# Sparse attention and a softplus feed-forward layer on one core: the second batch's attention in one TensorE visit a head pair, its masks on VectorE, and a new order of the first 140 microseconds

## The chip, the cores and the metric

The kernel runs on 1 core of one Trainium2 chip. The metric is device time in microseconds; the kernel before takes 890.61 us (median of 3 runs, 890.55 to 891.92). In the profile PE is TensorE, DVE VectorE, ACT ScalarE, POOL GpSimd and SP SyncE, which issues nearly all DMAs.

## The reference

Eight batches of eight heads, 576 tokens, head dimension 64. Heads 0 to 3 attend to the last 32 keys, heads 4 to 7 to earlier keys of the same class modulo 32. The attention output, 4608 tokens of 512 features, goes through a feed-forward layer with softplus:

```python
scores = scale * np.matmul(q, k.transpose(0, 1, 3, 2))
mask_local = (rel >= 0) & (rel < stride)
mask_strided = (rel >= 0) & (pos[None, :] % stride == pos[:, None] % stride)
scores = np.where(masks[None, :, :, :], scores, -1000000000.0)
attn = np.exp(scores - np.max(scores, axis=-1, keepdims=True))
attn = attn / (np.sum(attn, axis=-1, keepdims=True) + 1e-09)
x = attn @ v                      # to 4608 x 512
h = x @ w_in                      # 512 x 2048
g = np.maximum(h, 0.0) + np.log1p(np.exp(-np.abs(h)))
out = g @ w_out                   # 2048 x 512
```

All of it is float32; q and k are drawn so large that the softmax is sharp.

## The kernel before

**Pairs.** Two heads share the 128 partitions, so a batch is four pairs. Pair n is numbered through: 0 to 3 are the first batch, 4 to 7 the second, 8 and up the rest. For a pair: load q and k (`q`, `k`), lay q out in blocks with zeros between the two heads (`D`, a copy of half the partitions each), scores by matmuls of 64 columns (`S`, parts 0 and 1, six and three chunks of 64 keys), maxima (`X`), exponentials (`E`), sums, guard and reciprocals (`r`, `R`), normalisation (`M`), transposes of the probabilities, product with v (`V`, two halves), and the result split into a high and a low part (`H` on ScalarE, `L` on VectorE) that are stored as the columns of x.

**The exponentials** come in two forms. A narrow part takes one ScalarE instruction for each 64-wide chunk, with the maximum as bias (`x` prepares it) and the sum as a by-product. A wide part (named in `WIDE`, line 74) subtracts the maxima on VectorE (`Y`), takes one ScalarE instruction (`E`) and sums on VectorE (`Z`).

**Masks.** In batches 0 and 1 TensorE adds the masks: four matmuls of the identity with a mask tile a pair (line 340). From batch 2 on VectorE adds the mask while it moves the scores out of PSUM (`add_mask`, line 416).

**Transposes** of the first batch go over TensorE (`T`, three a pair) and are copied out of PSUM (`C`); all later ones are 16 VectorE stream transposes a pair (`P`, line 457).

**Feed-forward.** Tokens go in 9 chunks of 512. For chunk c and each of 16 blocks f of 128 hidden features: `F`, 12 matmuls of 512 columns (`hidden`, line 629: four column groups of x times high and low parts), three ScalarE passes (`A`, `Ae`, `Al`), softplus on VectorE (`u`), a high and a low part of the result (`Gh`, `Gl`), and `O`, 12 matmuls that add to four PSUM banks `py` (`output`, line 669). Each 128x512 block of weights arrives as 64-bit numbers (`wi`, `wo`) and is prepared once: `a` on ScalarE, `B` and `d` on VectorE, high part `h`, low part `l`.

**PSUM.** `ps_h` has two buffers, used by `F` (held until `u`), by `T` and by half of a joint product; `ps_o` and `ps_s` have one each.

**Order.** Up to the middle of the second chunk the order is written out by hand as the list `FIRST` (line 35): every engine gets its instructions, and SyncE its DMAs, in the order of the list; `ON_POOL`, `ON_VECTOR` and `ON_SCALAR` (lines 62 to 72) give the engine of the tasks that may go to several. `Fa` is the part of a hidden block that needs only the first three pairs, `F` then the rest. `Q`, `QA` and so on are the first two hidden blocks of chunk 1 (`Q` 0 and 1). Behind the list everything is ordered by the class `Plan`, from costs and due times: there one visit a pair (`S`) on TensorE does the scores of pair n, part 0 in `ps_s` and part 1 in `ps_o`, and the products of pair n-1 (`sums_of`).

In the second batch the four score parts and product halves of a pair are separate tasks of the list: TensorE goes there for S40, S41, S50, S51 with V40, V41 with S60, V50 with S61, V51 with S70, S71 with V60, V61, V70 and V71.

Of the kernel before, what the change touches and what calls it, by code (L numbers as in the profile page):

```python
# [18 lines left out]
P = 128  # L19
# [18 lines left out]
X20 T01 C01 Bo0 D30 v0 R1 do0 V00 H00 T02 C02 L00 Y20 M1 k3 S31 X31 E21 E20 Z20 V01 li0 wi1  # L38
S30 H01 L01 ai1 Bi1 r2 di1 x31 R2 M2 wi3 ai3 T10 C10 T11 C11 v1 T12 ho0 lo0 Bi3 V10 T21 X30 Y30
di3 C12 H10 L10 V11 E30 T20 E31 Z30 C21 H11 v2 L11 r3 R3 M3 C20 T22 wi2 ai2 Bi2 V20 C22  # L40
H20 L20 di2 hi3 li3 T32 k4 wo1 C32 wi9 T31 ao1 T30 C31 v3 C30 hi1 li1 V21 H21 wo2 ao2 L21 V31 wi4
V30 Bo1 Bo2 ai9 H31 L31 Fa0 q4 H30 L30 F0 wi10 do1 Bi9 di9 wo3 Fa1 hi2 li2 D4 S40 A0
Ae0 Al0 ho1 lo1 ao3 F1 u0 Gh0 X40 x40 F2 Bo3 Gl0 ai4 Bi4 hi9 li9 di4 do2 ho2 v4 A1 E40 S41
X41 x41 wi5 ai5 q5 Bi5 Ae1 Al1 u1 wo15 D5 lo2 O0 wi6 hi4 di5 li4 F3 Gh1 Gl1 O1 A2 Ae2 wi8 ai8
do3 ai10 k5 E41 S50 r4 hi5 wo12 Bi8 li5 Al2 A3 di8 u2 R4 Ae3 M4 Al3 wi7 ai7 wi12 hi8 X50
x50 F4 u3 Gh3 Bi10 di10 F5 Gh2 Gl2 wo5 wo4 ho3 lo3 E50 P4 O2 A4 Gl3 q6 hi10 ao5 Bo5 Ae4 Al4
u4 wi11 S51 A5 Ae5 li8 X51 li10 ai6 Al5 Bi7 di7 V40 H40 x51 Gh4 Gl4 E51 r5 F8 hi7 do5 u5 ao4
# [71 lines left out]
def attention_softplus_ffn(  # L119
# [201 lines left out]

    def scores(n, part):

        b = order[n][0]
        masked = b < 2
        if b == 0:
            ps = py[2 * (n % 2) + part]
        elif b == 1 or part == 0:
            taken.append(n)
            ps = ps_s.tile([P, 512], F32, tag="ps", name=f"ps_{n}_{part}")  # L330
        else:
            shared[n] = ps_o.tile([P, 512], F32, tag="po", name=f"po_{n}")
            ps = shared[n][:, S // 2 :]
        pss[n, part] = ps
        lo, hi = SPLIT[part]
        rows = [slice(64 * place, 64 * place + 64) for place in range(2)]

        def add(first):
            for place in range(2):
                nc.tensor.matmul(  # L340
                    ps[rows[place], : 64 * (hi - lo)],
                    lhsT=ident_b[:, rows[place]],
                    rhs=mask_of(n, part),
                    start=first,
                    stop=not first,
                )


        if masked and n > 0:
            add(True)  # L350
        for x in range(lo, hi):
            for place in range(2):
                a, i = block_at(x, place)
                c = TILE * a + 32 * i
                nc.tensor.matmul(  # L355
                    ps[rows[place], 64 * (x - lo) : 64 * (x - lo) + 64],
                    lhsT=blocks_of(n)[:, c // 32].rearrange("p h l -> p (h l)"),
                    rhs=k_of(n)[:, c : c + 64],
                    start=not masked or n == 0 and x == lo,
                    stop=not masked or n > 0 and x == hi - 1,  # L360
                )
        if masked and n == 0:
            add(False)
# [144 lines left out]
    def weighted(n, half, joint=False):  # L508


        if joint:
            if half == 0:
                po = shared[n + 1]
            else:
                po = ps_h.tile([P, 512], F32, tag="ph", name=f"pv_{n}")
        elif half == 1 and (n == NPAIR - 1 or n >= 2 * NPAIR):
            taken.append(n)
            po = ps_s.tile([P, 512], F32, tag="ps", name=f"pv_{n}_{half}")
        else:
            po = ps_o.tile([P, 512], F32, tag="po", name=f"pv_{n}_{half}")  # L520
        pos[n, half] = po
        for x in range(NTILE // 2):
            a = NTILE // 2 * half + x
            for h in range(2):
                nc.tensor.matmul(  # L525
                    po[64 * h : 64 * h + 64, TILE * x : TILE * x + TILE],
                    lhsT=vs[n][:, a, h, :],
                    rhs=pt_of(n, a)[:, h, a % 2],
                    start=True,
                    stop=True,  # L530
                )
# [170 lines left out]
    def of(name, usual):  # L702
# [7 lines left out]
    first["W"] = lambda: dummies(10)  # L710
    for n in range(2 * NPAIR + 2):
# [288 lines left out]
```

## Time and profile before

| what | value |
|---|---|
| time, median of 3 runs | 890.61 us (890.55 to 891.92) |
| span of the profiled execution, first to last instruction | 890.1 us |
| busy: TensorE | 879.0 us, 99% |
| busy: VectorE | 576.6 us, 65% |
| busy: ScalarE | 445.8 us, 50% |
| busy: GpSimd | 64.0 us, 7% |
| granted TensorE clock | 1.0 |
| DMA | 58.27 MB, mean 65 GB/s |

The page gives the profiled execution's own time as its span and no other. Busy shares are means over stages of different kinds: in the first tenth of the span ScalarE is at 9 tenths and the DMA engines above 5, in the last tenth both are at 3 or less. The views that are used are the windows (busy time of each engine in a stretch of time), the chain of waits (the work that ended last, followed back), the timelines of single engines, and the groups of instructions by line.

### The profile page before, as it was taken

The numbers are of one execution on the slowest core, as the hardware profiler recorded it, in microseconds if no ns is written. First come the engines' busy times: TensorE is split into PE (matmuls) and PEld (weight loads), VectorE is DVE, ScalarE is ACT, GpSimd is POOL, SyncE is SP. The second block draws the span as 40 slices with busy tenths as digits, with TensorE's granted clock in tenths as the row PEclk, the third lists the DMA queues.
The fourth block names the chain that finished last, engine by engine and source line by source line (L and its number), as shares of the span: only waits on it lengthen the run. The fifth ranks groups of instructions, "written<-read, shape, count | busy, mean of one in ns | idle before, by whom it ended". The sixth has DMA issues, their size and how long they took to land.

```text
span 890.1 us, 14332 instructions
## 1 busy us (share of the span) xinstructions
PE 879.0 (99%) x5634; PEld 723.6 (81%) x5634; DVE 576.6 (65%) x1268; ACT 445.8 (50%) x796; POOL 64.0 (7%) x93
## 2 busy tenths in 40 slices
PE   7999999999999999999999999999999999999998
PEld 5778888888888888888888888888888888888886
DVE  7878877788766777776766676677777333333332
ACT  7999665554544445445445454445543333333332
POOL 7254350000000000000000000000000000000000
PEclk9999999999999999999999999999999999999999
DMA  9856202121211122111211121111200010001001
GB/s 337 314 205 209 93 18 76 56 75 45 91 37 30 36 74 62 44 45 32 92 44 45 44 92 30 30 43 54 81 18 18 1 48 1 0 1 48 1 1 48
DMA packets 50083, 58.27 MB, mean 65 GB/s; under 512 B 3168, under 2 KB 35296, under 8 KB 50016
## 3 DMA queue, kind: packets, MB, share of 16 engines
q1 hardware_dynamic: 49728, 57.03, 19.5%
q8 instruction: 44, 0.72, 0.3%
q10 hardware_dynamic: 288, 0.33, 0.1%
q14 instruction: 23, 0.19, 0.1%
HBM read 47.91 MB, written 9.44 MB: 64 GB/s over the span
## 4 chain that ended last, share of the span: by engine, by line
PE 96%; ACT 2%; DMA 1%; DVE 1%; issue 0%; ACTq 0%
PE py L669 44%; PE ph L629 44%; PE ps L355 3%; PE pv L525 2%; PE po L525 1%; PE po L355 1%; DMA kT<-in_qk_dram 1%; PE idle L692 0%; ACT early_l L399 0%; ACT early_h L264 0%; ACT a_i L589 0%; ACT x_h L563 0%; ACT early_l L264 0%; PE py L355 0%; PE ps L340 0%
## 5 line engine op out<-in xcount | busy, mean ns | idle before, releaser
L669 PE MATMUL py<-w_o,gh 128*128 128x512 f32 x1152 | 358.4, 392 | 0.0
L629 PE MATMUL ph<-x_h,w_i 128*128 128x512 f32 x1152 | 355.5, 390 | 0.0
L641 ACT ACTIVATE u<-ph 128x512 f32<-128x512 f32 x144 | 86.3, 599 | 399.0 <-PE ph L629 398.6
L629 PEld LDWEIGHTS ph<-x_h,w_i 128*128 128x128 f32 x1152 | 215.7, 188 | 45.2
L669 PEld LDWEIGHTS py<-w_o,gh 128*128 128x128 f32 x1152 | 213.9, 188 | 46.4
L669 PE MATMUL py<-w_o,gl 128*128 128x512 f32 x576 | 224.1, 389 | 0.0
L629 PE MATMUL ph<-x_l,w_i 128*128 128x512 f32 x576 | 224.1, 389 | 0.0
L650 DVE SCALAR_TENSOR_TENSOR u<-ph,u 128x512 f32<-128x512 f32 x144 | 99.3, 690 | 178.3 <-ACT u L646 176.3
L457 DVE STREAM_TRANSPOSE pt<-prob 32x192 f32<-32x192 f32 x448 | 137.1, 314 | 6.4
L669 PEld LDWEIGHTS py<-w_o,gl 128*128 128x128 f32 x576 | 108.1, 188 | 22.8
L629 PEld LDWEIGHTS ph<-x_l,w_i 128*128 128x128 f32 x576 | 108.2, 188 | 22.6
L662 DVE TENSOR_TENSOR gl<-u,gh 128x512 fp32r<-128x512 f32 x136 | 94.3, 694 | 12.8 <-ACT gh L264 2.2
L644 ACT ACTIVATE u<-u 128x512 f32<-128x512 f32 x144 | 91.3, 634 | 4.3
L646 ACT ACTIVATE u<-u 128x512 f32<-128x512 f32 x144 | 91.1, 633 | 4.4
L264 ACT COPY qT<-prob 64x576 f32<-64x576 f32 x56 | 70.6, 1261 | 0.3
L264 DVE CAST gh<-u 128x512 fp32r<-128x512 f32 x128 | 54.5, 426 | 10.9 <-DVE u L650 0.5
L416 DVE TENSOR_TENSOR prob<-ps,mask_b 128x384 f32<-128x384 f32 x24 | 13.4, 558 | 50.0 <-PE ps L355 50.0
L355 PEld LDWEIGHTS ps<-kT,qT 128*64 128x64 f32 x720 | 24.0, 137 | 9.0 <-issue 8.5
L355 PE MATMUL ps<-kT,qT 128*64 128x64 f32 x720 | 27.6, 225 | 0.3 <-DMA kT<-in_qk_dram 0.3
L561 DVE TENSOR_TENSOR x_l<-pv,x_h 128x288 fp32r<-128x288 f32 (+2 forms) x47 | 18.8, 412 | 9.0 <-ACT x_h L563 8.9
L447 DVE TENSOR_TENSOR prob<-prob,st 128x576 f32<-128x576 f32 x27 | 21.9, 811 | 0.9
L525 PE MATMUL pv<-pt,v_in 128*64 128x96 f32 x396 | 22.1, 248 | 0.0
(100 smaller groups left out, 481.7 us busy)
## 6 DMA issues: line engine op xcount, KB each, us to landing
v_in<-in_v_dram SPq DMA_DIRECT2D x28, 320.0 KB, 3.5
out_dram<-o SPq DMA_DIRECT2D x35, 256.0 KB, 2.2
ri<-in_moe_w_in_dram SPq DMA_DIRECT2D x16, 512.0 KB, 7.3
ro<-in_moe_w_out_dram SPq DMA_DIRECT2D x16, 512.0 KB, 7.7
kT<-in_qk_dram SPq DMA_DIRECT2D x28, 288.0 KB, 2.9
prob<-in_qk_dram SPq DMA_DIRECT2D x28, 288.0 KB, 2.7
v_in<-in_v_dram SPq DMA_DIRECT2D x28, 48.0 KB, 2.7
room<-in_v_dram SPq DMA_DIRECT2D x4, 320.0 KB, 6.6
```

The source lines that it names most:

```text
L264: (engine.copy if engine is nc.scalar else engine.tensor_copy)(dst, src)
L355: nc.tensor.matmul(ps[rows[place], 64 * (x - lo) : 64 * (x - lo) + 64], lhsT=blocks_of(n)[:, c // 32].rearrange("p h l -> p (h l)"), rhs=k ...
L447: engine.tensor_tensor(pv, pv, rc.unsqueeze(2).broadcast_to(pv.shape), op=ALU.mult)
L457: nc.vector.transpose(pt[32 * (i + c) : 32 * (i + c) + 32, h, a : a + hi - lo, 32 * i : 32 * i + 32,], src[:, lo:hi, 32 * c : 32 * c + 32],)
L525: nc.tensor.matmul(po[64 * h : 64 * h + 64, TILE * x : TILE * x + TILE], lhsT=vs[n][:, a, h, :], rhs=pt_of(n, a)[:, h, a % 2], start=True, ...
L629: nc.tensor.matmul(ph, lhsT=w32["i", f][:, half, cc * P : (cc + 1) * P], rhs=x_of(x, cc)[:, t0 : t0 + n], start=(i == 0), stop=(i == 3 * N ...
L641: nc.scalar.activation(us[c, f], phs[c, f], AF.Abs)
L644: nc.scalar.activation(u, u, AF.Exp, scale=-1.0)
L646: nc.scalar.activation(u, u, AF.Ln, bias=1.0)
L650: nc.vector.scalar_tensor_tensor(u, in0=phs.pop((c, f)), scalar=0.0, in1=u, op0=ALU.max, op1=ALU.add)
L662: engine.tensor_tensor(g, us.pop((c, f)), ghs[c, f].bitcast(F32), op=ALU.subtract)
L669: nc.tensor.matmul(py[t], lhsT=g[:, sl], rhs=w32["o", f][:, half], start=(f == 0 and n == 0), stop=(f == NFC - 1 and n == 2),)
```

## The change

The list `FIRST` and the lists of engines are replaced; nothing in `Plan` changes. In words:

- Second batch: the masks are added by VectorE (`Y`, `add_mask`), not by TensorE; one maximum over all nine chunks (`X4` for pair 4), one preparation of the bias (`s4`), nine narrow exponentials from SBUF. One task `J` does both score parts of a pair and the products of the pair before it; pair 7's products stay `V70` and `V71`.
- First batch: wide parts are 00, 10, 20, 30, 01 and 21 in place of 00, 11, 20 and 30.
- Hidden blocks 0 to 3 are cut into `Fa` and `F`, before only 0 and 1.
- The second half of the products of pairs 0 to 3 and 7 goes to `ps_s`, before of pair 3 and of those from 8 on.
- The zeros for the layout of pair 4's q are a task (`z4`) and no longer part of the setup; the layouts of pairs 4 to 8 are two tasks each, so that the halves can go to different engines.
- Engines: 35 tasks on GpSimd (33 before), 42 on VectorE (29 before); the order of all tasks is new.

```diff
-W mask q0 D00 k0 D01 S00 X00 Y00 q1 D11 S01 X01 E00 x01 Z00 k1 D10 S11 X11 q2 D20 Y11 E01 r0 wi0
-S10 X10 D21 x10 k2 S21 ai0 wo0 q3 D31 S20 R0 M0 E10 Bi0 di0 X21 hi0 E11 T00 x21 C00 ao0 Z11 r1
...
+q0 k0 mask D00 W q1 q2 k1 D01 k2 D11 S00 D21 S01 D10 X00 X01 D20 q3 Y00 E00 Y01 S10 z4 E01 X10 Z00
+Z01 D30 k3 S11 X11 D31 r0 S21 Y10 S20 wi0 x11 R0 M0 S30 T00 X21 E10 X20 wi2 ai0 T01 E11 v0 Z10 Y20
+r1 Y21 X30 E20 v2 C00 C01 R1 Z20 M1 E21 ai2 Y30 Z21 S31 T02 V00 C02 X31 E30 H00 r2 v1 Bi0 wi1 T11
+T10 C11 Bi2 C10 R2 x31 Z30 V01 L00 T12 E31 di0 V10 H01 ai1 C12 L01 M2 T20 T21 r3 v3 R3 C20 H10 M3
+hi0 V11 Bi1 wi3 T22 C21 T31 wi4 H11 C22 L10 L11 di1 C31 wo2 hi1 V20 V21 k4 wi5 T30 wo0 T32 di2 ai3
+H20 H21 L20 C30 L21 C32 li1 q4 ao2 li0 V30 V31 H31 hi2 wi15 ai4 Bi3 di3 Fa0 wo1 Bi4 wi8 li2 hi3 L31
+H30 ai5 q5 L30 F0 di4 hi4 Bi5 Fa1 A0 Ae0 Bo2 wi6 D40 li3 Al0 ao0 wo5 F1 u0 li4 di5 D41 A1 do2 Ae1
+Bo0 wi11 Fa2 Al1 do0 Gh0 J4 ho2 hi5 ho0 wo4 u1 F2 Y41 lo2 li5 lo0 Gl0 ao1 D50 Y40 A2 ai6 Bo1 Fa3 k6
+Gh1 Ae2 wi9 Al2 ai8 X4 do1 wo8 Gl1 O0 u2 ao5 Bo5 F3 s4 wo9 Bi8 k5 E4 wo3 v4 wi7 ho1 Bi6 A3 Gh2 lo1
+do5 Ae3 F4 Al3 D51 Gl2 di6 di8 ho5 wo7 r4 hi6 O1 R4 hi8 u3 F5 li8 ao4 M4 Gh3 P4 A4 Gl3 wi10 Ae4 Al4
+u4 Bo4 wi13 A5 O2 do4 Ae5 Al5 li6 ai7 Bi7 J5 ao3 Bo3 q6 u5 v5 wo14 lo5 ho4 di7 F8 H41 do3 Gh5 Y50
+Y51 Gh4 wi14 hi7 ao8 wi12 Gl5 li7 X5 O5 L41 ho3 H40 ao7 lo4 A8 ai11 lo3 Bo8 F6 Ae8 s5 Bo7 do8 Gl4
+Al8 Bi11 ai9 D60 wo10 di11 E5 wo6 u8 hi11 A6 r5 Ae6 do7 Gh8 Bi9 ho8 Al6 F7 L40 R5 M5 Gl8 di9 lo8 O4
+wo11 u6 ai10 li11 ho7 A7 D61 Ae7 O3 P5 hi9 ai12 Al7 lo7 ao6 J6 Bi12 Bo6 di12 H51 li9 u7 do6 H50 Y61
...
 WIDE = """
-00 11 20 30
+00 10 20 30 01 21
 """.split()
...
-    for n in range(NPAIR + 1):
-        zeros(n)
+    for n in range(NPAIR):
+        zeros(n, nc.vector if n < 2 else nc.gpsimd)
...
-        b = order[n][0]
-        masked = b < 2
-        if b == 0:
+        masked = n < NPAIR
+        if masked:
             ps = py[2 * (n % 2) + part]
-        elif b == 1 or part == 0:
+        elif part == 0:
...
+    def row_exponentials(n):
+
+        pv, _, (mx, sm, _, _) = parts(n)
+        for a in range(NCHK):
+            nc.scalar.activation(
+                pv[:, a],
+                pv[:, a],
+                AF.Exp,
+                bias=mx[:, a : a + 1],
+                scale=SCALE,
+                accum_out=sm[:, a : a + 1],
+            )
...
-        elif half == 1 and (n == NPAIR - 1 or n >= 2 * NPAIR):
+        elif half == 1 and (n < NPAIR or n >= 2 * NPAIR - 1):
...
+    def joint_scores(n):
+
+        scores(n, 0)
+        scores(n, 1)
+        if n > NPAIR:
+            for half in range(2):
+                weighted(n - 1, half, True)
...
+            task(f"J{n}", joint_scores, n)
+            for j in range(2):
+                task(f"Y{n}{j}", add_mask, n, j)
+            task(f"X{n}", row_maxima, n)
+            task(f"s{n}", bias_of, n, None, of(f"s{n}", nc.vector))
+            task(f"E{n}", row_exponentials, n)
...
-        if f < 2:
+        if f < 4:
             task(f"Fa{f}", hidden, 0, f, range(3))
             task(f"F{f}", hidden, 0, f, range(3, 4))
```

More of the change, by code (lines that the diff above doesn't have):

```diff
@@ L35 @@
 FIRST = """
-W mask q0 D00 k0 D01 S00 X00 Y00 q1 D11 S01 X01 E00 x01 Z00 k1 D10 S11 X11 q2 D20 Y11 E01 r0 wi0
-S10 X10 D21 x10 k2 S21 ai0 wo0 q3 D31 S20 R0 M0 E10 Bi0 di0 X21 hi0 E11 T00 x21 C00 ao0 Z11 r1
[L38 to L47, printed above, removed]
@@ L60 @@
+ai15 q8 Bi15 F11 O9 Al10 A11 u10 Ae11 ao12 Al11 di15 J7 Bo12 hi15 u11 li13 Gh11 D80 do12 ao11 ho12
+H61 F14 Y70 L61 lo12 Gl11 Gh10 A14 Y71 Gl10 D81 X7 s7 E7 O12 Bo11 F13 ao13 li15 Ae14 A13 Bo13 do13
+Al14 Ae13 H60 Al13 k8 r7 O10 do11 u14 F15 L60 ho11 u13 Gh13 ho13 lo11 ao15 Bo15 R7 Gl13 A15 O11 M7
+P7 Ae15 k9 Al15 Gh14 lo13 Qa0 v7 do14 ho14 lo14 Gl14 O13 do15 V70 H70 V71 H71 ho15 u15 L71 O14 L70
+v8 Gh15 lo15 Gl15 Q0 Q1 QA0 Qu0 QA1 Qh0 O15 Ql0 q9 y1 Qu1 Ob15 y0 y2 y3 Qh1 Ql1
 """
 ON_POOL = """
-D10 D20 x10 D31 hi0 x21 r2 x31 r3 hi3 hi1 ho1 Gh0 ho2 x41 hi4 r4 x50 x51 x60 Gh6 x61 r6 ho8 ho10
@@ L64 @@
-ho9 x71 r7 hi14 hi15 ho13 ho14 ho15
+D21 D30 r0 x11 r1 r2 x31 r3 hi0 hi1 hi2 hi4 D40 Gh0 ho2 s4 Gh2 ho5 Gh3 ho4 Gh5 hi7 D60 hi11 r5 ho8
+hi9 hi12 hi10 hi14 D80 D81 s7 Gh14 ho14
 """.split()
 ON_VECTOR = """
-D01 M0 C00 M3 li3 li1 li2 lo1 Gl0 li9 lo2 li4 Gl1 Gl4 li6 lo6 Gl6 lo7 Gl7 li12 lo8 M6 Gl9 lo11
-li14 M7 lo13 Gl14 Gl15
+D00 D10 C12 M3 li1 li0 hi3 li3 li4 hi5 lo0 Gl0 Gh1 Gl1 ho1 Gl2 hi8 li8 Gl5 li7 lo3 Gl4 M5 lo8 Gh6
+ho6 lo6 Gh9 li14 D71 Gl9 lo10 li13 lo12 Gl11 lo11 lo14 Gl14 ho15 lo15 Gl15 y0
```

57 lines of the change are left out of this document (24 added, 33 removed).

## The prediction

> **What bounds the kernel now.** I read the page first, then windows cut where the stages change, then the chain of waits, then each engine's timeline. Span and windows (columns: us, then busy time and instructions of PE, PEld, DVE, ACT, POOL, granted clock, DMA share, GB/s):
>
> ```profile
> span 890.1 us, 14332 instructions
> ...
> 0.00:30.51 30.51, 23.56 (x483) 18.36 (x483) 24.21 (x52) 24.45 (x67) 19.18 (x46) 1.00 0.90 309
> 30.51:139.73 109.22, 108.97 (x678) 87.44 (x680) 86.10 (x186) 89.33 (x205) 44.86 (x47) 1.00 0.46 159
> 139.73:886.24 746.51, 746.50 (x4476) 617.77 (x4476) 465.86 (x1029) 331.65 (x524) 0.00 (x0) 1.00 0.13 41
> ...
> 4.17:30.51 26.34, 20.57 (x477) 17.30 (x475) 21.78 (x47) 22.88 (x65) 15.85 (x32) 1.00 0.95 330
> ```
>
> From 30.51 us, when the first block Fa0 starts, TensorE is busy without a gap (109.22 us with 0.25 idle, then 746.51 with none). So the time is the start of Fa0, plus the matmuls behind it, plus any gap that the change opens. Everything from 139.73 (score visit S8) on is written by the planner, which the change leaves alone. Two stages can move: up to 30.51, and 30.51 to 139.73. Chain of waits (start, us, what):
>
> ```profile
> 30.51 4.99 PE ph L629 x21
> 35.50 0.28 PE ps L340 x2
> 35.78 0.70 PE ps L355 x24
> 36.48 3.67 PE ph L629 x15
> ...
> 43.64 2.72 PE ph L629 x12
> ...
> 124.56 0.65 PE pv L525 x12
> 125.21 2.96 PE py L669 x12
> ...
> 157.47 0.85 PE ps L355 x24
> 158.32 0.35 PE po L355 x12
> 158.67 0.50 PE po L525 x12
> 159.17 0.49 PE pv L525 x12
> 159.66 2.94 PE py L669 x12
> ```
>
> A block of twelve wide matmuls takes 2.72; the first one behind a visit of small matmuls takes 2.94 to 2.96, so a switch costs 0.23. Visit S40 costs 0.28 for masks, 0.70 for scores and 0.27 for the switch (3.67 against 15 x 0.227). A visit of one half's products costs 0.65 + 0.24. The planner's joint visit, which the second batch now copies, costs 0.85 + 0.35 + 0.50 + 0.49 + 0.22 = 2.41.
>
> **Part 1: TensorE visits.** Before, 30.51 to 139.73 holds 35 blocks: 18 of hidden and 16 of output in the first two chunks, and the planner's F18. 35 x 2.72 = 95.2, so the 11 visits and the first switch take 109.22 - 95.2 = 14.0. After, the order has J4 (scores alone: 0.85 + 0.35 + 0.23 = 1.43), J5 to J7 (3 x 2.41), V70 with V71 (0.65 + 0.49 + 0.23 = 1.37) and the first switch 0.23: 10.3. Gain **3.7**, of which the 16 removed mask matmuls are 4 x (0.28 + 0.20) = 1.9. Cutting hidden blocks 2 and 3 in two adds no switch: J4 stands at one cut, more wide matmuls at the other.
>
> **Part 2: up to Fa0.** What is late before is pair 3:
>
> ```profile
> 12.43 1.23 POOL L264 COPY early_h<-raw_q 64x576 f32<-64x576 f32 x1 [0.71 <-DMA raw_q<-in_qk_dram]
> ...
> 15.42 1.27 ACT L264 COPY early_h<-raw_q 64x576 f32<-64x576 f32 x1
> ...
> 25.14 1.08 DVE L447 TENSOR_TENSOR prob<-prob,st 128x576 f32<-128x576 f32 x1
> ...
> 12.62 1.75 ACT early_l L399 x12
> 14.37 0.25 ACT early_l L381
> ...
> ri<-in_moe_w_in_dram SPq DMA_DIRECT2D x16, 512.0 KB, 7.3
> ...
> raw_q<-in_qk_dram SPq DMA_DIRECT2D x4, 288.0 KB, 4.8
> ```
>
> D31 waits until 12.43 for q3; D30 stands at 15.42 in ScalarE's queue behind nine narrow exponentials; so pair 3 is normalised (M3) only at 25.14. After, SyncE issues q3 ahead of wi0 and wo0: 1.05 MB less in front of it, at 330 GB/s 3.2 us, so it lands near 9.3. D30 goes to GpSimd (behind D21 and z4, 1.6 of memset that used to stand in the setup), D31 to ScalarE: both end near 10.8. S30 can run once Y10 has left py, about 11.2.
>
> Two more wide parts: a narrow column costs ScalarE 0.29 (1.75 for six), a wide part 0.43 or 0.25. Narrow columns fall from 15 to 6 (-2.6), wide ones cost 0.7 more: ScalarE -1.9, VectorE +1.5 for a subtract and a sum each. Summing the list ahead of Fa0 with the steps between starts in the timelines: ScalarE 17.8 (4 D x 1.24, exponentials 4.0, 5 weight scalings x 0.60, 11 C x 0.37, 6 H x 0.30) against 22.5 before; VectorE 18.4 (2 D 1.8, maxima 3.0, subtracts 2.6, sums 2.4, 6 L 2.3, weights 4.2, rest 2.1) against 20.1. From 4.17, at the busy shares of that window (ScalarE 22.88/26.34 = 0.87, VectorE 0.83), they end at 24.7 and 26.4. Followed by hand from wait to wait, it ends with C32, V31 and li0 at 25.3. I take Fa0 at **26.0**, 4.5 earlier; the ends are 25.3 and no gain, since the DMA engines are at 0.95 here and every move may queue behind another. By bytes, what Fa0 needs (eight loads of q or k, 0.29 MB each, four of v, wi0 and the two blocks of weights between) is in by 20 us, and wo0, first needed 11 us behind Fa0, by 28. SyncE's new order has q4 wait for pair 3's transposes (T32, 23.9 by hand), with wi15, wo1 and wi8 behind it, and v5 for J5, with wo14, wi14, wi12 and wo10 behind it; none of these is needed within 12 us, so I cost both at nothing. If that cover went, a block of weights would be late by what is left of its 7.3 us from issue to landing.
>
> **Part 3: does VectorE keep up?** This is what I weigh most. The masks move to VectorE (Y 0.50 + 0.30 and one maximum of 0.72 a pair, for 0.75 of maxima before), and it takes 42 listed tasks instead of 29.
>
> ```profile
> 31.85:57.47 25.62, 21.04 (x47) 1.00 0.68 248
> 57.47:75.36 17.89, 14.97 (x36) 1.00 0.58 202
> 75.36:101.03 25.67, 23.27 (x51) 1.00 0.44 152
> ...
> L457 DVE STREAM_TRANSPOSE pt<-prob 32x192 f32<-32x192 f32 x448 | 137.1, 314 | 6.4
> L650 DVE SCALAR_TENSOR_TENSOR u<-ph,u 128x512 f32<-128x512 f32 x144 | 99.3, 690 | 178.3 <-ACT u L646 176.3
> L264 DVE CAST gh<-u 128x512 fp32r<-128x512 f32 x128 | 54.5, 426 | 10.9 <-DVE u L650 0.5 <-PE py L669 0.5
> L416 DVE TENSOR_TENSOR prob<-ps,mask_b 128x384 f32<-128x384 f32 x24 | 13.4, 558 | 50.0 <-PE ps L355 50.0
> L416 DVE TENSOR_TENSOR prob<-po,mask_b 128x192 f32<-128x192 f32 x24 | 8.6, 358 | 19.3 <-ACT x_h L563 19.3
> L421 DVE TENSOR_REDUCE st<-prob 128x9 f32<-128x576 f32 x24 | 17.9, 745 | 0.0
> ...
> 76.43 0.42 DVE L593 TENSOR_SCALAR a_o<-a_o 128x512 uint32<-128x512 uint32 x1
> 76.77 0.68 DVE L650 SCALAR_TENSOR_TENSOR u<-ph,u 128x512 f32<-128x512 f32 x1
> ...
> 88.41 0.69 DVE L600 SCALAR_TENSOR_TENSOR a_o<-ro,a_o 128x512 uint32<-128x512 uint32 x1
> 89.02 0.68 DVE L650 SCALAR_TENSOR_TENSOR u<-ph,u 128x512 f32<-128x512 f32 x1
> ```
>
> (The three windows are of VectorE alone.) One after the other, instructions start 0.08 sooner than the last one's time is over (88.41 to 89.02: 0.61 of 0.69; 76.43 to 76.77: 0.34 for a B, 0.45 where its d comes next). From L30, the last thing that F0 needs, to u7, which frees the PSUM buffer of F9 behind J6, the new list gives VectorE 16 d, 7 l, 5 Gl and 9 u (37 x 0.61 = 22.6), 16 B (0.38: 6.1), two P (16 transposes, 4.9 each: 9.8) and the masks, maxima and casts (6.9): 45.4. The same prices for L30 to P6 before give 56.3, and the windows show 59.28 busy, 5% more; I take 4%: 47.2. In front u0 waits 0.6 for F0's rest and three passes of ScalarE. So F9 can't start sooner than 47.8 behind L30. TensorE's own work there: 0.68 + 14 blocks (38.1), J4, J5 and J6 before its switch (1.43 + 2.41 + 2.19): 44.8. So VectorE is the bound by **3.0**; the wait shows at J5 to F8 (P4, u5) and at J6 to F9 (P5, u7), with the planned blocks queued behind them. Before, its list for L30 to P5 held 34 us of work in a stretch of 43.5, and TensorE never waited for it. Behind u7 the slack comes back: 36 of VectorE's work up to P7 stand against 46 of TensorE's, so no more stalls. ScalarE has 40 in the same stretch: hidden.
>
> ```profile
> L662 DVE TENSOR_TENSOR gl<-u,gh 128x512 fp32r<-128x512 f32 x136 | 94.3, 694 | 12.8 <-ACT gh L264 2.2
> L615 DVE TENSOR_TENSOR w_o<-a_o,w_o 128x512 fp32r<-128x512 f32 x7 | 5.5, 791 | 0.4 <-POOL w_o L264 0.4
> ```
>
> One form, two operands in SBUF, costs 694 mostly with GpSimd idle and 791 while it works; what this cost before is in the 5%. The Trainium skill ("SBUF — State Buffer", Who interferes with whom) says that GpSimd and a VectorE instruction with two SBUF inputs or in a two-port mode shut each other out for the whole instruction. By the list GpSimd would be busy 28 of these 48 us, 0.58 against the 0.41 of 30.51 to 139.73 before (44.86 of 109.22), so by that rule the surcharge would be some 8% and the forecast 1.7 later; the rows show the surcharge, not whose lock it is.
>
> **The sum.** Fa0 26.0; L30 2.55 later (Bi3, di3, Bi4, hi3, L31, L30: 2.5): 28.55; F9 47.8 later: 76.35; then its switch 0.23, 20 blocks (54.4), J7 2.41 and V7 1.37 to S8: 134.8 against 139.73, -4.9. VectorE's and ScalarE's other waits I put at 0.8: between nothing (behind P5, 75.36 on, it ran seven us with no idle) and the pace of before (below). 890.1 - 4.1 = 886.0 of span. The runs' median, 890.61, lies 0.5 above the span: **886.5**, with 884.5 to 888.7 its own range.
>
> **The rivals.**
> - VectorE keeps up, TensorE stays gapless. For it: it waited 176 us for ScalarE's u in the whole run, so its queue mostly runs ahead. Against: the sum above. Fa0 at 25.3 gives -5.2 - 3.7: 881.7.
> - The lead-in doesn't shorten (DMA share 0.95; li0, C32 and V31 come late). Fa0 at 30.5, L30 33.05, F9 80.85, S8 139.25, with the 0.8: +0.3, so 890.9: no change, as VectorE's stall eats the visits' gain.
> - Slower: VectorE holds only the pace of before, 59.28 busy of 69.18 = 0.857, as each wait for ScalarE or GpSimd in its fixed order now counts. 47.2/0.857 = 55.1 behind L30: F9 at 83.65, S8 at 142.05, +2.3: 892.9. It decides from a pace of 0.894 (52.8 us) down. For it: 0.857 is measured. Against: these waits were mostly for a TensorE that was not yet there, and a queue that is behind doesn't have them.
>
> That the visits are not saved isn't a rival: the mask matmuls are gone from the code, and the order holds five visits.
>
> **How the numbers follow.** Likeliest 0.42, VectorE keeps up 0.20, no shorter lead-in 0.18, slower 0.20. A measurement of this kernel tells some 0.2% (1.8 us) from no change. Faster: 0.39 + 0.20 = 0.59; same: 0.03 + 0.15 + 0.03 = 0.21; slower: 0.03 + 0.17 = 0.20. The range goes from the second case to the last: 881.5 to 893.0.
>
> **What would show it.** Fa0's start near 26 and not 30.5; S8 near 135.6; five visits, 10.3 us with switches; TensorE idle 3 to 4 us between J5 and F9, released by VectorE's transposes (L457) and u (L650); VectorE busy over 95% there. No idle time there gives the first rival; Fa0 at 30 the second; over 8 us of idle time the third. A wait for weights' DMA would be none of them, and I would be wrong altogether.

## The result and the profile after

The kernel after takes **903.14 us** (median of 4 runs, 902.27 to 903.37) against 891.26 us before (4 runs on the same chip, 890.55 to 891.98): ratio 1.0126, 95% interval 1.0112 to 1.0141. It is 11.9 us slower; the prediction was 886.5, with a range up to 893.0.

Span, then windows of the kernel after, cut at its Fa0, at the block F9, and at the score visit S8 (columns: us, then busy time and instructions of PE, PEld, DVE, ACT, POOL, granted clock, DMA share, GB/s):

```profile
span 901.2 us, 14291 instructions
...
0.00:27.00 27.00, 21.86 (x483) 17.59 (x483) 21.60 (x48) 20.32 (x46) 17.31 (x46) 1.00 0.98 330
...
27.00:85.00 58.00, 49.85 (x338) 38.38 (x337) 56.60 (x109) 42.31 (x97) 30.55 (x29) 1.00 0.66 229
85.00:150.87 65.87, 60.42 (x326) 47.68 (x328) 51.75 (x104) 38.51 (x93) 21.96 (x19) 1.00 0.23 76
150.87:897.37 746.50, 746.50 (x4476) 617.77 (x4476) 465.86 (x1029) 331.64 (x524) 0.00 (x0) 1.00 0.14 40
```

The last window is the old one to the hundredth (746.50, no idle time), so all of the loss lies ahead of S8. That visit starts at 150.87 in the chain of waits, 11.14 later than the 139.73 of before; the span grew by 11.1:

```profile
150.87 0.85 PE ps L351 x24
```

Fa0 starts 3.51 earlier. Behind it TensorE, which had 0.25 us of idle time before, now waits again and again. Its timeline (start, us, what, and in brackets the idle time before it and what ended that):

```profile
27.00 0.74 PE L638 MATMUL ph<-x_h,w_i 128*128 128x512 f32 x2
...
39.26 0.73 PE L638 MATMUL ph<-x_h,w_i 128*128 128x512 f32 x2 [1.10 <-DVE u L659]
...
61.31 0.73 PE L638 MATMUL ph<-x_h,w_i 128*128 128x512 f32 x2 [1.56 <-DVE u L659]
...
72.20 0.70 PE L638 MATMUL ph<-x_h,w_i 128*128 128x512 f32 x2 [1.28 <-POOL w_i L261]
...
85.00 0.70 PE L638 MATMUL ph<-x_h,w_i 128*128 128x512 f32 x2 [1.38 <-POOL w_i L261]
...
89.24 0.70 PE L638 MATMUL ph<-x_h,w_i 128*128 128x512 f32 x2 [1.27 <-DVE x_l L570]
```

From 27.00 to 150.87 are 123.87 us. The 35 blocks take 95.2 and the visits, by the prediction's sum, 10.3; so **18.4 us are waits**, where 3.8 were forecast. Adding up the timeline's 17 gaps of more than 0.25 us gives 16.8. (A gap is counted here from one matmul's start to the next one's, less the 0.23 us that a wide matmul takes in an unbroken row, or 0.05 for a small one; the brackets count from the modelled end of the matmul and are some 0.2 smaller.) No single wait is above 1.8. The two lines whose bracket names GpSimd's w_i, 72.20 and 85.00, are waits for `u` as well: those casts are the high parts of blocks 11 and 12, which the matmuls behind the gaps (F7 and F9) don't read, and these start 0.15 us behind the end of u8 and u7, as Fa2 does behind u0 at 33.76. No gap ends on a DMA. VectorE is busy 56.60 of the 58.00 us up to F9 (0.98): it is the bound, as forecast, but with more time than its list was priced at. That time shows in VectorE's groups by shape, here of the kernel after between 27 and 115 us (count, then busy us, mean ns of one, and idle time before):

```profile
L609 DVE SCALAR_TENSOR_TENSOR a_i<-ri,a_i 128x512 uint32<-128x512 uint32 x13 | 10.7, 831 | 0.1
L609 DVE SCALAR_TENSOR_TENSOR a_o<-ro,a_o 128x512 uint32<-128x512 uint32 x12 | 10.2, 847 | 0.1
L659 DVE SCALAR_TENSOR_TENSOR u<-ph,u 128x512 f32<-128x512 f32 x13 | 8.9, 683 | 1.7 <-ACT u L655 1.6
...
L624 DVE TENSOR_TENSOR w_i<-a_i,w_i 128x512 fp32r<-128x512 f32 x6 | 7.2, 1204 | 0.0
L602 DVE TENSOR_SCALAR a_i<-a_i 128x512 uint32<-128x512 uint32 x13 | 6.6, 508 | 0.4 <-ACT a_i L598 0.4
L602 DVE TENSOR_SCALAR a_o<-a_o 128x512 uint32<-128x512 uint32 x13 | 6.3, 482 | 0.0
...
L624 DVE TENSOR_TENSOR w_o<-a_o,w_o 128x512 fp32r<-128x512 f32 x5 | 5.7, 1143 | 0.0
L671 DVE TENSOR_TENSOR gl<-u,gh 128x512 fp32r<-128x512 f32 x6 | 5.0, 840 | 0.0
L261 DVE CAST w_i<-a_i 128x512 fp32r<-128x512 f32 x3 | 2.3, 764 | 0.0
...
L261 DVE CAST gh<-u 128x512 fp32r<-128x512 f32 x3 | 2.0, 677 | 0.0
L261 DVE CAST w_o<-a_o 128x512 fp32r<-128x512 f32 x2 | 1.9, 955 | 0.0
```

The same view of the kernel before, between 30 and 105 us:

```profile
L600 DVE SCALAR_TENSOR_TENSOR a_o<-ro,a_o 128x512 uint32<-128x512 uint32 x11 | 7.6, 689 | 0.1
L600 DVE SCALAR_TENSOR_TENSOR a_i<-ri,a_i 128x512 uint32<-128x512 uint32 x10 | 7.1, 717 | 0.2
...
L593 DVE TENSOR_SCALAR a_i<-a_i 128x512 uint32<-128x512 uint32 x11 | 4.8, 441 | 0.4 <-ACT a_i L589 0.4
L593 DVE TENSOR_SCALAR a_o<-a_o 128x512 uint32<-128x512 uint32 x11 | 4.8, 445 | 0.2
L662 DVE TENSOR_TENSOR gl<-u,gh 128x512 fp32r<-128x512 f32 x6 | 4.4, 735 | 1.0 <-ACT gh L264 1.0
L615 DVE TENSOR_TENSOR w_o<-a_o,w_o 128x512 fp32r<-128x512 f32 x5 | 4.2, 832 | 0.0
L615 DVE TENSOR_TENSOR w_i<-a_i,w_i 128x512 fp32r<-128x512 f32 x5 | 4.1, 820 | 0.2 <-ACT w_i L264 0.2
```

The same instruction became dearer: d from 689 to 847 ns, the low part l of output weights from 832 to 1143, of input weights from 820 to 1204. `u`, which has one operand in PSUM, stayed at 683 (688 before). Against undisturbed prices (d and gl 684, l 692, B 420, a cast 400, all from rows of the experiments below) the excess over these groups is, after: d 20.9 - 25 x 0.684 = 3.8, l 12.9 - 11 x 0.692 = 5.3, gl 0.9, B 12.9 - 26 x 0.42 = 2.0, casts 6.2 - 8 x 0.40 = 3.0, together **15.0 us**; before 0.3 + 1.4 + 0.3 + 0.4 = **2.4 us**. That is 22% and 4% on top of VectorE's other work in these two windows.

What is beside the long ones? VectorE's timeline of the kernel after, then GpSimd's:

```profile
31.26 1.75 DVE L624 TENSOR_TENSOR w_i<-a_i,w_i 128x512 fp32r<-128x512 f32 x1
...
46.56 1.78 DVE L609 SCALAR_TENSOR_TENSOR a_o<-ro,a_o 128x512 uint32<-128x512 uint32 x1
```

```profile
31.01 1.45 POOL L261 COPY qT<-prob 64x576 f32<-64x576 f32 x1
...
46.44 1.35 POOL L624 TENSOR_TENSOR w_o<-a_o,w_o 128x512 fp32r<-128x512 f32 x1 [0.76 <-DMA ro<-in_moe_w_out_dram]
```

GpSimd's copy ends at 32.46, and VectorE's l, issued at 31.26, is over at 33.01, 0.55 later; at 46.44 likewise (47.79 and 48.34). Each looks as if it had stood still until GpSimd was through, and then taken 0.55, somewhat less than the 0.69 that it takes alone.

### The profile page after: what moved, and what is told of

Its sections match the earlier page's. It is cut to its first block, busy times and chain, and to the rows that moved or that the text cites. A ratio compares the mean times of both kernels' runs of the same rounds, so it can differ in the third digit from the quotient of the medians.

```text
span 901.2 us, 14291 instructions
## 1 busy us (share of the span) xinstructions
PE 878.6 (97%) x5618; PEld 721.4 (80%) x5618; DVE 596.2 (66%) x1289; ACT 433.1 (48%) x760; POOL 69.8 (8%) x94
## 4 chain that ended last, share of the span: by engine, by line
PE 86%; DVE 5%; DMA 3%; issue 2%; ACT 2%; POOL 1%; SPq 1%; POOLq 0%; DVEq 0%; ACTq 0%
PE py L678 40%; PE ph L638 39%; PE ps L351 2%; PE pv L534 2%; PE po L534 1%; DVE pt L466 1%; PE po L351 1%; DMA ro<-in_moe_w_out_dram 1%; DMA kT<-in_qk_dram 1%; DMA early_l<-in_qk_dram 1%; DMA ri<-in_moe_w_in_dram 1%; DVE a_i L609 1%; PE pt L504 1%; DVE w_o L624 0%; DVE u L659 0%
## 5 line engine op out<-in xcount | busy, mean ns | idle before, releaser
L678 PEld LDWEIGHTS py<-w_o,gh 128*128 128x128 f32 x1152 | 214.3, 188 | 47.8 <-DVE w_o L624 1.4
L671 DVE TENSOR_TENSOR gl<-u,gh 128x512 fp32r<-128x512 f32 x137 | 96.8, 706 | 11.1 <-DVE gh L261 0.5
L261 ACT COPY qT<-prob 64x576 f32<-64x576 f32 x51 | 64.2, 1259 | 0.3
L261 DVE CAST gh<-u 128x512 fp32r<-128x512 f32 x131 | 56.5, 432 | 10.1
L412 DVE TENSOR_TENSOR prob<-ps,mask_b 128x384 f32<-128x384 f32 x28 | 15.6, 556 | 49.4 <-PE ps L351 49.4
L351 PEld LDWEIGHTS ps<-kT,qT 128*64 128x64 f32 x672 | 21.9, 137 | 9.9 <-issue 9.2
L351 PE MATMUL ps<-kT,qT 128*64 128x64 f32 x672 | 25.7, 226 | 0.0
L412 DVE TENSOR_TENSOR prob<-po,mask_b 128x192 f32<-128x192 f32 x28 | 10.0, 356 | 19.3 <-ACT x_h L572 19.3
L572 ACT CAST x_h<-pv 128x288 fp32r<-128x288 f32 (+2 forms) x44 | 15.6, 371 | 13.7 <-PE pv L534 13.5
L417 DVE TENSOR_REDUCE st<-prob 128x9 f32<-128x576 f32 x28 | 20.9, 746 | 0.1
```

The lines of the kernel that those rows point to most:

```text
L261: (engine.copy if engine is nc.scalar else engine.tensor_copy)(dst, src)
L351: nc.tensor.matmul(ps[rows[place], 64 * (x - lo) : 64 * (x - lo) + 64], lhsT=blocks_of(n)[:, c // 32].rearrange("p h l -> p (h l)"), rhs=k ...
L412: nc.vector.tensor_tensor(pv, sv, m, op=ALU.add)
L671: engine.tensor_tensor(g, us.pop((c, f)), ghs[c, f].bitcast(F32), op=ALU.subtract)
L678: nc.tensor.matmul(py[t], lhsT=g[:, sl], rhs=w32["o", f][:, half], start=(f == 0 and n == 0), stop=(f == NFC - 1 and n == 2),)
```

## The experiments

**GpSimd without its reads.** In the kernel after, GpSimd's high and low parts behind the setup read only 4 columns and fill the rest with zeros; this part of the computation is left out, while VectorE's and all other work stays.

```diff
+    def pool_write(dst, src, times):
+        nc.gpsimd.tensor_copy(dst[:, :4], src[:, :4])
+        for _ in range(times):
+            nc.gpsimd.memset(dst[:, 4:].bitcast(F32), 0.0)
...
+        if engine is nc.gpsimd:
+            return pool_write(w32[w, f][:, 0], part[w, f].bitcast(F32), 1)
```

> The changed kernel, but where GpSimd makes a high or low part of weights or of the softplus result it now reads four columns of its input and writes zeros over the rest (once for a high part, twice for a low part); those parts of the result are left out. Waits, order and VectorE's instructions are the same, GpSimd reads next to nothing. Theory A (VectorE and GpSimd shut each other out while GpSimd reads): between 27 and 115 us VectorE's d goes from 0.84 back to 0.69 on average, its l from 1.18 to about 0.70; TensorE's waits, 16.8 us in the changed kernel, fall below 8, and the time falls from 903 to 889 to 895. Casts and B may stay slow, if writing counts for them. Theory B (the list simply gives VectorE too much, or waits for ScalarE and DMA do it): VectorE's durations matter little; the time stays within 3 us of 903.

Measured: **891.36 us**, ratio to the kernel before 0.9997 (0.9985 to 1.0008). VectorE between 27 and 105 us, and the chain:

```profile
L614 DVE SCALAR_TENSOR_TENSOR a_o<-ro,a_o 128x512 uint32<-128x512 uint32 x12 | 8.2, 684 | 0.1
...
L633 DVE TENSOR_TENSOR w_i<-a_i,w_i 128x512 fp32r<-128x512 f32 x6 | 5.3, 890 | 0.0
L684 DVE TENSOR_TENSOR gl<-u,gh 128x512 fp32r<-128x512 f32 x6 | 4.1, 683 | 0.0
L633 DVE TENSOR_TENSOR w_o<-a_o,w_o 128x512 fp32r<-128x512 f32 x5 | 3.5, 692 | 0.0
```

```profile
138.61 0.85 PE ps L356 x24
```

and in TensorE's timeline the block F9:

```profile
76.48 0.70 PE L647 MATMUL ph<-x_h,w_i 128*128 128x512 f32 x2 [0.47 <-DVE u L668]
```

With GpSimd as busy as in the kernel after (45.5 us of the 83.3 up to 110) but writing instead of reading, d, gl and the low part of output weights cost their bare price, the excess on VectorE falls from 15.0 to 4.0 us, and the time by 11.8. So the whole loss against the kernel before goes with GpSimd's reads. What remains lies on low parts beside the layouts of q and the normalisations, which GpSimd still reads, and on casts and B, which stay dearer beside writes too. The other half of the finding: even then there is **no gain**. Fa0 is at 26.68, so 138.61 - 26.68 - 105.5 = 6.4 us of waits still eat the shorter lead-in and the saved visits.

**The lock by itself.** In the kernel before, GpSimd is idle from 139.73 on. Here it gets extra work beside `gl`: two copies that read for blocks 40 to 64, two memsets for blocks 65 to 89, nothing else.

```diff
+        if 40 <= i < 65:
+            nc.gpsimd.tensor_copy(scratch[:, : CH[c]], g)
+            nc.gpsimd.tensor_copy(scratch[:, : CH[c]], g)
+        elif 65 <= i < 90:
+            nc.gpsimd.tensor_copy(scratch[:, :4], g[:, :4])
+            nc.gpsimd.memset(scratch, 0.0)
+            nc.gpsimd.memset(scratch, 0.0)
```

> The disputed cost by itself: the kernel before, with extra GpSimd work in the steady stage, where GpSimd otherwise does nothing. Behind each high part of the softplus result GpSimd copies it twice to a scratch tile in steps 40 to 64; in steps 65 to 89 it reads four columns and writes zeros twice. Theory A: in the first of the two stages the low part gl (two operands in SBUF) goes from 0.69 to 1.1 or more whenever a copy runs beside it, in the second it stays at 0.69; u (one operand in PSUM) and the transposes stay as they are in both. Theory B: gl stays at 0.69 in both. The time should stay within 2 us of the kernel before, as VectorE has room there.

Measured, as three windows of one profile (300 to 420 us with copies, 440 to 560 with memsets, 600 to 700 with neither):

```profile
L662 DVE TENSOR_TENSOR gl<-u,gh 128x512 fp32r<-128x512 f32 x20 | 19.3, 967 | 1.7
...
L439 DVE TENSOR_SCALAR st<-st 128x9 f32<-128x9 f32 x5 | 2.4, 484 | 0.2
```

```profile
L662 DVE TENSOR_TENSOR gl<-u,gh 128x512 fp32r<-128x512 f32 x20 | 13.8, 692 | 1.7
...
L439 DVE TENSOR_SCALAR st<-st 128x9 f32<-128x9 f32 x5 | 2.7, 547 | 0.2
```

```profile
L662 DVE TENSOR_TENSOR gl<-u,gh 128x512 fp32r<-128x512 f32 x16 | 11.1, 692 | 1.3
...
L439 DVE TENSOR_SCALAR st<-st 128x9 f32<-128x9 f32 x4 | 0.7, 174 | 0.1
```

`gl`, with two operands in SBUF, goes from 692 to 967 beside reads and stays at 692 beside writes; the tiny guard, a tensor_scalar of 9 columns, about trebles beside both. The transposes cost the same in all three (370 and 259), and 12 of them ran beside the copies. `u` (689 in all three) never stood beside a copy here, but in the kernel after 6 of its 13 ran beside GpSimd's work, at 681 to 685. The timeline of the first window, GpSimd and VectorE together, shows what happens to `gl`:

```profile
302.51 0.62 POOL L669 COPY scratch<-gh 128x512 f32<-128x512 f32 x1 [3.56 <-DVE gh L264]
302.55 1.12 DVE L662 TENSOR_TENSOR gl<-u,gh 128x512 fp32r<-128x512 f32 x1
303.19 0.95 POOL L670 COPY scratch<-gh 128x512 f32<-128x512 f32 x1
```

The copy that starts first takes 0.62; `gl` ends 0.54 behind it; the second copy, issued while `gl` still runs, ends 0.47 behind `gl`. Where `gl` started first (314.80, ahead of a copy at 314.83) it kept its 0.69 and the copy took 1.14. The time of the whole kernel is 890.7 us, one run beside 891.7 of the kernel before: in this stage VectorE has slack, and the lock costs nothing.

**Taking work off GpSimd.** Three variants of the kernel after move its work behind F0: its 17 casts to ScalarE; these and VectorE's 8 casts to ScalarE; all of it, casts to ScalarE, low parts and normalisations to VectorE. The first:

```diff
 ON_POOL = """
-D21 D30 r0 x11 r1 r2 x31 r3 hi0 hi1 hi2 hi4 D40 Gh0 ho2 s4 Gh2 ho5 Gh3 ho4 Gh5 hi7 D60 hi11 r5 ho8
-hi9 hi12 hi10 hi14 D80 D81 s7 Gh14 ho14
+D21 D30 r0 x11 r1 r2 x31 r3 hi0 hi1 hi2 D40 s4 D60 r5 D80 D81 s7
 """.split()
```

> The changed kernel with GpSimd's 17 high parts behind block F0 on ScalarE, where a good third of the time is free; GpSimd keeps the low parts, the layouts and the normalisations, VectorE's list is the same. Theory A: GpSimd reads some 10 us less between 27 and 115 us, VectorE's surcharge there falls from about 15 to 9 to 11 us: 897 to 900. Theory B: VectorE's list is as long as it was, and ScalarE gets longer: 903 or more.

Measured 899.36 us (ratio 1.0093, 1.0076 to 1.011), 3.8 below the kernel after. VectorE's casts fall to some 400 ns and B to 427, the excess to 8.6 us (27 to 110 us). What is left is d, l and gl beside GpSimd's remaining low parts.

> The changed kernel with all 25 casts behind the first hidden block that stood on GpSimd (17) or VectorE (8) on ScalarE; the run with GpSimd's 17 alone moved took 899.4 us with a surcharge of 8.8 us on VectorE. Theory A (VectorE sets the end, by its own work and by its surcharge from GpSimd): the 8 casts take 3.4 us of VectorE's own work and their part of the surcharge away, 894 to 897 us. Theory B (ScalarE, with 25 x 0.6 = 15 us more than in the changed kernel, becomes what TensorE waits for): 899 us or more, and TensorE's waits are released by ScalarE or by work that stands behind its casts.

Measured 902.50 us (1.0114, 1.0097 to 1.0131): 2.6 us dearer than with 17 casts moved, each taken against its own runs of the kernel before, although the excess falls further, to 6.9. VectorE has 12.7 us of idle time between 27 and 112, in place of 4.4 between 27 and 115 after; 5.4 of them end on a cast on ScalarE. TensorE waits for one too:

```profile
49.43 0.50 PE L678 MATMUL py<-w_o,gh 128*128 128x512 f32 x1 [0.84 <-ACT w_o L261]
```

> The changed kernel with GpSimd empty behind block F0: its 21 low parts and 3 normalisations go to VectorE, its 17 high parts and 4 layouts to ScalarE, its small ones to VectorE; the order is the same. Theory A (mutual exclusion is what costs): although VectorE's list grows by some 15 us of work, from L30 to u7 from 45.4 to about 53, every instruction now takes its undisturbed time, d and B included; TensorE's waits fall from 18 to 8 to 12 us, 893 to 898. Theory B (VectorE's list is what is too long): more work on VectorE makes it worse, 908 or more.

Measured 911.86 us (1.0234, 1.0219 to 1.0249). The excess is gone (at most 0.2 us), but VectorE has 21 low parts more, and TensorE's single waits for it get longer:

```profile
91.46 1.19 PE L639 MATMUL ph<-x_h,w_i 128*128 128x512 f32 x2 [3.19 <-DVE u L660]
```

So the lock is not cured by emptying GpSimd in this order. Why it costs 8.7 us more than the kernel after is not separated. TensorE's gaps add up to 18.8 us, only 2 more than in the kernel after; but its granted clock is 0.92 on average from 27 us to S8 at 160.75, against 1.00 there, which is some 10 us of full-speed time (the last section tells of the clock behind long pauses). ScalarE got more work here too.

**One visit a pair, in the order of before.** The code of the kernel after with the lists of before; the tokens of the second batch are replaced where they stand, and J6 and J7 set where their products are ready. In the first version u5 stood too late; the second moves it, and hi14. Parts of two lines of the list, against the kernel before:

```diff
-hi2 li2 D4 S40 A0
+hi2 li2 D40 D41 J4 A0
...
-Ae0 Al0 ho1 lo1 ao3 F1 u0 Gh0 X40 x40 F2 Bo3 Gl0 ai4 Bi4 hi9 li9 di4 do2 ho2 v4 A1 E40 S41
+Ae0 Al0 ho1 lo1 ao3 F1 u0 Gh0 Y40 Y41 X4 s4 Fa2 F2 Bo3 Gl0 ai4 Bi4 hi9 li9 di4 do2 ho2 v4 A1 E4
```

> One part of the change alone: the order, engines and wide parts of the kernel before, but the second batch in one visit a pair (J4 where S40 stood, J5 where V40, J6 behind block O5, J7 where S71, V70 with V71) with masks on VectorE. Theory A: GpSimd's work and what VectorE does beside it are as before, so TensorE waits for VectorE at most 2 us, and the visits' 3.7 us come through: Fa0 at 30.5, 887 to 889. Theory B (products that wait inside a visit, or VectorE's load of masks, stall TensorE): 892 or more with over 4 us of new waits at J5, J6 and J7.

> The one visit a pair and VectorE's masks alone, in the order of the kernel before, with u5 directly behind J5 (it stood behind the exponentials of pair 5, and TensorE waited 5.9 us for it) and the high part of weights i14 ahead of pair 7's guard (2.5 us). Theory A: the two waits and the half clock behind them go, some 12 to 14 us; what is left of waits at J5 to J7 decides: 890 to 896. If one visit a pair were a gain by itself in this order, 888 or less; if its products always come too late, over 898.

Measured 908.55 us (1.0191, 1.0175 to 1.0206), then **904.01** (1.0142, 1.0127 to 1.0157). The first is dominated by one wait of 5.7 us for u5 and says little. In the second the excess on VectorE is only 3.8 us, and yet many waits of 0.8 to 2.4 us stand behind the visits, for high and low parts of weights and for u. So the saved TensorE time isn't a gain by itself either: with the masks and a joint maximum on VectorE, these two orders, which weren't made for it, lose 13 us or more with little of the lock. Whether another order would keep the gain is not shown.

**The lead-in alone.** The kernel before with the changed order up to F0, the six wide parts and the second half of the first batch's products in `ps_s`; from F0 on its own order, in six placings of what follows (from the third on the high and low part of output weight 0 also change their engine). The new lead-in is shorter in part because it puts work off: the preparation of output weight 0, parts of those of output weights 1 and 2 and one low part, which the kernel before does ahead of F0, come behind it, and parts of input weights 2, 4 and 5 come ahead in their place. In the kernel after, with the same lead-in, VectorE is busy 21.60 us ahead of Fa0, before 24.21. The first placing (-) and the fifth (+):

```diff
-L31 H30 ai5 q5 L30 F0 li3 ao0 Bo0 do0 ho0 lo0 wi9 ao1 Bo1 Bo2 do2 ho2 lo2 ai9 wi10 do1 Bi9 di9 wo3
-Fa1 D4 S40 A0 Ae0 Al0 ho1 lo1 ao3 F1 u0 Gh0 X40 x40 F2 Bo3 Gl0 hi9 li9 di4 v4 A1 E40 S41 X41 x41
+L31 H30 ai5 q5 L30 F0 li3 Fa1 D4 A0 Ae0 Al0 S40 ao0 F1 u0 Gh0 X40 x40 Bo0 do0 ho0 A1 F2 E40 lo0
+Gl0 Ae1 Al1 S41 X41 x41 u1 O0 wi9 ao1 Gh1 Bo1 do1 ho1 Gl1 lo1 Bo2 A2 do2 ho2 Ae2 wo15 lo2 Al2 wi10
```

> One part of the change alone: its order, engines and wide parts up to block F0, behind it the rest of the tasks in the order and on the engines of the kernel before, with four score and product visits a pair and masks on TensorE. Theory A: Fa0 at 27.0 as in the changed kernel, and as the rest has the GpSimd work of before, most of the 3.5 us comes through: 887 to 889. Theory B (an earlier start only meets engines that are behind): TensorE waits 3 us or more before 140 us, 890 to 893.

> The change's order up to block F0 alone, as before, but behind F0 the layout of pair 4's q, its score visit and the passes of block 0 now stand ahead of the preparation of weights o0, o2 and o9, which blocked ScalarE's queue in front of them (TensorE waited 8.3 us for that layout and then ran at half clock for 3 us). Theory A: Fa0 at 27.0 and no wait over 1 us behind it: 887 to 889. Theory B: the rest of the order isn't ready 3.5 us earlier: 890 or more.

> The kernel before with the changed lead-in alone, a third placing of what follows the first hidden block: the exponentials of pair 4's first part stand ahead of the preparation of output weights 1 and 2, so that the score visit S41 no longer waits 8.3 us for them; masks stay on TensorE and the visits of the second batch stay separate. Theory A (the 4 us of the lead-in are kept where nothing behind it waits; what the two earlier placings lost was their one long wait): first hidden block at about 27.3, no wait of TensorE over 2 us behind it, score visit S8 at 136 to 138, 886 to 889.5 us. Theory B (VectorE and ScalarE have the same work to do behind a start that is 3 us earlier, and the wait only moves): a wait of 2 us or more somewhere before 80 us, 891 us or more.

> The kernel before with the changed lead-in alone, as in the third placing, but with output weight 1 ahead of output weight 2 and the high and low part of the second hidden block's result ahead of the input weights 4 and 5 on ScalarE and VectorE: in the third placing the second output block waited 2.5 us for that low part and ran at half the rate for 3 us behind the pause. Theory A (the shorter lead-in is kept where nothing behind it waits): S8 at 136 to 138, no pause of TensorE over 1.5 us, 887 to 890 us, below the kernel before. Theory B (the engines behind the lead-in have no reserve for a start that is 3 us earlier, so the wait moves on): a pause of 2 us or more at another place before 80 us, 892 us or more.

> The kernel before with the changed lead-in alone, as in the fourth placing, but with the ScalarE passes of hidden blocks 2 and 3 and their u ahead of the weights that stood in front of them: in the fourth placing one visit waited 4.7 us for u2, behind a ScalarE pass that stood at 49.5 us. Theory A (the shorter lead-in is kept where nothing behind it waits): no pause of TensorE over 1.5 us, S8 at 136 to 138, 887 to 890 us. Theory B (no reserve behind the lead-in, the wait moves on): a pause of 2 us or more before 80 us, 892 us or more.

> The kernel before with the changed lead-in alone, as in the fifth placing, but with the high and low part of input weight 5 right behind those of weight 4: in the fifth placing TensorE waited 1.7 and 0.9 us for these two parts, which stood behind passes and weights that were needed later. Theory A (the shorter lead-in is kept where nothing behind it waits): no pause of TensorE over 1.5 us, S8 at 136 to 138, 887 to 890 us. Theory B (VectorE and ScalarE have no reserve for a start that is 3 us earlier, whatever their order): a pause of 1.5 us or more at another place before 80 us, 891 us or more.

| placing | time, us | ratio to before, 95% | longest wait of TensorE |
|---|---|---|---|
| first | 898.88 | 1.006 to 1.0093 | 8.3 us, S40 for the layout of q behind weights |
| second | 901.14 | 1.0095 to 1.0125 | 8.3 us, S41 for exponentials behind weights |
| third | 894.01 | 1.0015 to 1.0035 | 2.5 us, for gl |
| fourth | 895.53 | 1.0034 to 1.0061 | 4.7 us, F4 for u2 |
| fifth | 894.32 | 1.0021 to 1.0046 | 1.7 us, for a cast of weights |
| sixth | 896.16 | 1.0024 to 1.0052 | 2.3 us for exponentials, 1.9 for u |

One wait of each of four of them, in TensorE's timelines of the second, third, fourth and sixth placing:

```profile
47.41 0.37 PE L339 MATMUL ps<-mask_b,ident_b 128*64 128x192 bf16 x2 [8.30 <-ACT prob L398]
```

```profile
46.81 0.50 PE L668 MATMUL py<-w_o,gl 128*128 128x512 f32 x1 [2.51 <-DVE gl L661]
```

```profile
51.03 1.19 PE L628 MATMUL ph<-x_h,w_i 128*128 128x512 f32 x2 [4.69 <-DVE st L442]
```

```profile
62.94 1.22 PE L628 MATMUL ph<-x_h,w_i 128*128 128x512 f32 x2 [1.87 <-DVE u L649]
```

(The third of these lines is F4's wait for u2: the bracket names the event that came last, and F4 starts 0.15 us behind the end of u2.) Theory A's numbers were missed six times; each repair took its wait away and another came up. In the first placing the sum nearly closes: Fa0 at 27.15 is 3.4 earlier, the pause costs 8.6 from start to start, the stretch at half clock behind it some 2, and S8 comes 7.1 later (146.85); from 60 to 150 us TensorE is busy 90.00 of 90.00. So there the head start isn't eaten slowly, but lost at one task that wasn't ready. That it wasn't ready because it is now needed 3 to 5 us earlier, with the put-off work ahead of it, is a reading that no run separates from the placing itself. Whether some order keeps the head start stays open; none of these six beats the kernel before.

## Why the prediction was wrong

- **Fa0** (Part 2): forecast 26.0, measured 27.00. Right but for 1 us; the products of pair 3 stand on TensorE directly ahead of it until then, and li0 was ready at 26.71.
- **Visits** (Part 1): 10.3 forecast. The gaps that add up to 16.8 leave at most 1.6 us for dearer visits and small gaps. The term stands.
- **The surcharge on VectorE** (Part 3) is the step that failed: "the windows show 59.28 busy, 5% more; I take 4%". For the kernel before 4% was right (2.4 us). After, it is 22% (15.0 us), and without GpSimd's reads the time falls by 11.8. In that run F9 starts at 76.48, 47.2 behind the end of L30 (29.26); the forecast was 76.35, 47.8 behind. So the prices of the list and the path over u7 to F9 were right, and the surcharge is the term that was mis-sized. The prediction took the surcharge for a property of the instructions and carried it over as a share. It hangs on which instructions run side by side. Going through both timelines one by one, 3 of 21 d and 3 of 10 l stood for 0.1 us or more beside work of GpSimd before, 11 of 25 and 8 of 11 after; before, 43 of 48 transposes, which aren't slowed, ran beside GpSimd, and after 30 of 48. Who had begun first counts too: the d and l that VectorE began ahead of GpSimd's instruction (after, at 33.54, 42.90, 61.18 and 74.86) kept their 675 to 678 ns, and two of GpSimd's casts behind them took 1.01 and 0.94 in place of 0.61.
- The rule that the prediction weighed there, of the Trainium skill ("SBUF — State Buffer", Who interferes with whom), that an instruction of VectorE with two SBUF inputs and a reading GpSimd exclude each other, and that two-port forms contend with GpSimd altogether, agrees with the runs: 967 against 692 beside reads, 692 beside writes; 484 and 547 against 174 for the guard. The forecast made from it (8%, 1.7 us) was too small, since it scaled the surcharge by GpSimd's busy share, and that only went from 32.00 of 73.49 us (0.44) to 42.87 of 88.00 (0.49).
- **F9**: 47.8 us behind L30 forecast; L30 ends at 29.7, and F9 starts at 85.00, 55.3 later. The slower rival gave 55.1 for this stretch, which is luck, as it came by another mechanism: it had VectorE waiting at a pace of 0.857, and VectorE was busy 0.98 of it. Its work got longer; it didn't idle.
- **"Behind u7 the slack comes back: ... so no more stalls"** failed too: from F9 to S8 58.5 us were forecast, 65.87 were measured. Without GpSimd's reads it is still 62.1 (76.48 to 138.61), so about half of this miss isn't the lock's. VectorE is busy only 51.75 of the 65.87, but what it does comes too late for the buffers: at 89.24 F12 waits for x_l, which frees the PSUM buffer of J6's product, behind a cast that took 1.50 beside GpSimd.
- The signs to look for were 3 to 4 us of idle TensorE between J5 and F9. There were 5.9 (gaps of 1.76, 0.57, 1.44, 0.52 and 1.58). The places that were named, u5 behind J5 and P5 and u7 behind J6, held 3.9 of them, as forecast; the rest of the 16.8 came where none was forecast: 2.0 for gl and u8 in between, 3.6 ahead of J5, and some 7 from F9 on.

## What to carry to other kernels

Price an instruction of VectorE with two SBUF operands twice, alone and beside a reading GpSimd, and count from the two orders how often they will meet; a busy share doesn't tell that. Where VectorE is the bound, its transposes and PSUM reads are what can stand beside GpSimd's work at no extra price; an order made that way was not tried here. And a shorter lead-in or a saved visit on TensorE is only worth what the other engines have ready by the earlier time: here over 7 us of saved time (3.8 of lead-in, 3.7 of visits) gave none even with GpSimd's reads out of the way.

## What the runs showed of the hardware

The lock is whole, and both sides lose: the one that starts second waits. GpSimd's two copies of 128x512 beside `gl` took 0.79 and 0.84 us on average, where the one that starts first takes 0.62, and single instructions of VectorE in the kernel after went up to 1.79, 2.6 times their price.

TensorE's clock was halved for some 3 us behind most of its pauses of 2 us or more, and where it was, the wait cost 1.5 us or so more than its length. Windows behind the pauses of the second placing (8.30) and the sixth (1.87 in the bracket, 2.07 from one matmul to the next beyond its own time); the granted clock is the third number from the end:

```profile
47.41:50.80 3.39, 3.39 (x20) 2.79 (x20) 2.34 (x5) 3.35 (x4) 0.90 (x2) 0.50 0.14 58
```

```profile
62.94:65.94 3.00, 3.00 (x7) 2.42 (x8) 2.97 (x7) 2.92 (x10) 1.08 (x2) 0.50 1.04 354
```

In the kernel after, whose pauses stay below 1.8, the clock is 1.00 throughout, so nothing of its loss comes from there. Length alone doesn't decide between 1.8 and 2.4 us: pauses of 1.9 and 2.0 us in two other runs didn't halve the clock, nor did one of 2.4 in the second run with one visit a pair, while a pause of 1.8 followed by one of 1.2 in the fifth placing did. The Trainium skill ("TensorE: Matmul & The Clock Gate", Why this matters for your kernels) advises no idle gaps above about 3 us; here 2.1 were enough once, so the measurement decides.
